# Key-value products of a linear attention: two matmuls of 64 weight columns in place of four of 32

## The chip, the cores and the metric

The kernel runs on one core of a Trainium2 chip. The metric is the time of one execution on the device in microseconds (us). A core has TensorE (PE in the profile; its weight loads are listed apart, as PEld), VectorE (DVE), ScalarE (ACT), GpSimd (POOL) and SyncE (SP), which here issues the DMA transfers. Each engine works through its own list of instructions in order and waits for the others at semaphores.

## The reference, cut to what matters

Three layers follow each other: a linear attention with exponential features, a mixer with Fourier transforms and a two-layer network, and a second mixer. The change touches the first, of which this is the core:

```python
def phi(x):
    proj = np.einsum('bhsd,df->bhsf', x, w_phi)
    proj = proj - np.max(np.abs(proj), axis=-1, keepdims=True)
    return np.concatenate([np.exp(proj), np.exp(-proj)], axis=-1)
q_p, k_p = (phi(q), phi(k))
kv = np.einsum('bhsf,bhsd->bhfd', k_p, v)
z = np.sum(k_p, axis=2)
num = np.einsum('bhsf,bhfd->bhsd', q_p, kv)
den = np.einsum('bhsf,bhf->bhs', q_p, z)[..., None] + 1e-06
return (num / den).astype(np.float32)
```

There are 4 batches, 8 heads, 576 tokens, 64 values a head, and 128 features of each sign. `kv` is the product that the change rewrites.

## The kernel before, in words

The 32 pairs of batch and head are worked off in 8 super-units `i` of four heads each: two heads stand one above the other on the partitions (index `j`), and two more along the tokens (index `u`). For each super-unit `a_load` and `a_loadv` fetch keys, queries and values. `a_proj` (L435) projects 128 tokens at a time onto the 128 features, VectorE takes the largest magnitude (L440) and subtracts it (L442), and for the keys ScalarE makes the two exponentials `ek` (L452), one for each sign `s`. `a_kv` then multiplies: the weights are `ek` of one tile of 128 tokens (128 features), the moving operand is `v` of that tile, 64 values and a column of ones that gives `z`, 65 columns. The tile that holds tokens of both heads is taken first, with 130 columns. So the first half of a super-unit (`u = 0`) makes 4 products of 130 columns and 16 of 65, the second half (`u = 1`) 16 of 65; all add up in PSUM tiles `pk`, one for each `j`. `kv_mm` (L457 to L459) is the product itself. `a_kz` copies the sums to SBUF (L486). Queries are projected likewise, turned by TensorE (L498, L510) and exponentiated (L503, L518); `a_den` (L531) makes the denominators with weights of 32 columns, `a_num` (L551) the numerators with weights of 64 columns. Behind them stand the division (`a_div`), the Fourier stages (`f_fold`, L625, L641, L673), and the layer norm `ln`, whose sum over the features is a matmul with ones (L915). From about 226 us the two networks and the second mixer follow (L1010, L1032 to L1034, L1102, L1111).

Nothing is scheduled by a compiler here: `ORDER` and `PRM` are tables that give every step a time, `at` and `later` put the steps into a heap by these times, and the heap is emptied in order. The times only set the order in which each engine gets its instructions. Steps of the weight preparation for the later layers (`w_ahead`, L718 to L781, L1564) stand among the attention's on VectorE, ScalarE, GpSimd and SyncE. When the last key-value products have released their memory, `w_fetch` (L805) loads the first network's weights.

All operands of `kv_mm` are full float32, and the compiled program executes each such matmul as two weight loads and two matmul records.

Of the kernel before, what the change touches and what calls it, by code (L numbers as in the profile page):

```python
# [270 lines left out]
def mixer_kernel(ctx: ExitStack, tc: tile.TileContext, qT, kT, vt, wphi, w11, w12, wt1, wt2, w21, w22,  # L271
                 dcos, dsin, scos, ssin, outT):
    nc = tc.nc
# [181 lines left out]
            later(V('d2', 0.8) + V('d6', 0.6) * j, sub, j)  # L455

    def kv_mm(out, e, v, first, last):  # L457
        for g in range(0, 128, 32):
            nc.tensor.matmul(out[g:g + 32], e[:, g:g + 32], v, start=first, stop=last)  # L459

    def a_kv(i, u):
        need(("v", i))
        if u:
            need(("kv", i, 0))
        elif i:
            need(("kz", i - 1, 0), ("kz", i - 1, 1))
        mark("kv", i, u)
        v, vs = T["v", i]
        if u == 0:
            T["kv", i] = [pk() for _ in range(2)]  # L470
            for j in range(2):
                for s in range(2):
                    kv_mm(T["kv", i][j][:, s * 130:s * 130 + 130], T["ek", i, j, 0][:, 0, s, :], vs[:, j], s == 0, False)
        for n in range(4):
            t = 1 + 4 * u + n
            for j in range(2):
                for s in range(2):
                    o = s * 130 + u * 65
                    kv_mm(T["kv", i][j][:, o:o + 65], T["ek", i, j, t // 4][:, t % 4, s, :], v[:, t - 1, j * 65:j * 65 + 65],
                          False, u == 1 and s == 1 and n == 3)  # L480
# [862 lines left out]
    last = {}  # L1343
# [190 lines left out]
    v = -1  # L1534
# [88 lines left out]
```

## Time and profile before

| | us |
|---|---|
| median of three runs | 1012.09 |
| the three runs | 1012.09, 1011.25, 1015.5 |
| the profiled execution | 1015.1 |
| its span, first to last instruction | 1013.4 |
| TensorE busy | 976.6 (96%) |
| VectorE, ScalarE, GpSimd busy | 694.6, 429.0, 409.4 |

The profile is of one execution. A row of the timeline gives the start, the length and the number of records merged in it, and in square brackets how long the engine had been idle before it and what ended that; "issue" is written where the wait ended with nothing that the profile shows. The view of stretches gives, for each engine, busy time and the number of its instructions. [...] Instructions themselves come from memory over DMA queues of their own, which the list of queues shows as "instruction".

### The profile page before, as it was taken

How to read it: one execution, taken by the hardware profiler on the slowest of the kernel's cores; microseconds unless marked ns; L12 is line 12 of the kernel's file. 1: busy time of each engine (PE TensorE's matmuls, PEld its weight loads, DVE VectorE, ACT ScalarE, POOL GpSimd, SP SyncE). 2: the span in 40 equal slices, each digit the busy share in tenths (PEclk: the TensorE clock that was granted, in tenths of full speed). 3: DMA queues.
4: the chain of work that ended last, by engine and by line, in shares of the span. 5: the costliest groups of instructions: out<-in, count | busy, mean ns of one | idle time of the engine just before them, and what ended most of it. 6: DMA issues, size and time to landing. Idle time of an engine off the chain costs nothing.

```text
span 1013.4 us, 23531 instructions
## 1 busy us (share of the span) xinstructions
PE 976.6 (96%) x9468; PEld 907.7 (90%) x9468; DVE 694.6 (69%) x1285; ACT 429.0 (42%) x954; POOL 409.4 (40%) x430
## 2 busy tenths in 40 slices
PE   7898999899999999999999999999999999999997
PEld 6666777579998899999999999988899999999996
DVE  5787998689689864544756753357666767766666
ACT  3676565463233422222323332234354446544442
POOL 0142223104124631523444752323266568865652
PEclk9999999899999999999999999999999999999999
DMA  8648474714445742565552498880035555754442
GB/s 283 188 138 262 134 267 155 272 40 137 169 157 178 216 163 79 197 238 181 196 170 96 162 372 334 252 293 2 1 114 170 164 177 158 244 161 146 146 146 94
DMA packets 97208, 178.66 MB, mean 176 GB/s; under 512 B 9300, under 2 KB 53268, under 8 KB 93516
## 3 DMA queue, kind: packets, MB, share of 16 engines
q1 hardware_dynamic: 97100, 177.16, 51.7%
q8 instruction: 75, 1.23, 0.5%
q14 instruction: 33, 0.27, 0.1%
HBM read 126.39 MB, written 48.31 MB: 172 GB/s over the span
## 4 chain that ended last, share of the span: by engine, by line
PE 85%; DVE 9%; issue 3%; ACT 1%; POOL 1%; DMA 0%; DVEq 0%; ACTq 0%; POOLq 0%
PE pw L1010 18%; PE pw L1102 12%; PE pz L1111 11%; PE pw L435 4%; PE pk L459 4%; PE pa L551 4%; PE pk L1033 3%; PE pk L1034 3%; PE pa L1032 3%; PE pk L1032 3%; PE pa L1034 3%; PE pa L1033 3%; PE pw L673 2%; DVE t L1564 2%; PE pa L531 2%
## 5 line engine op out<-in xcount | busy, mean ns | idle before, releaser
L1010 PE MATMUL pw<-xh,w 128*128 128x288 f32 x896 | 197.0, 295 | 0.0
L1166 DVE TENSOR_TENSOR u<-u,pz 128x576 f32<-128x576 f32 x158 | 118.9, 753 | 61.4 <-PE pz L1111 59.4
L1102 PE MATMUL pw<-x,ring 128*128 128x288 f32 x1008 | 155.4, 297 | 3.8 <-DVE f L1124 3.8
L1111 PE MATMUL pz<-g,ring 128*128 128x288 f32 x984 | 152.1, 298 | 1.5 <-DVE y L1161 1.0
L1010 PEld LDWEIGHTS pw<-xh,w 128*128 128x128 f32 x896 | 150.1, 188 | 0.5 <-DVE c L942 0.4
L1018 DVE SCALAR_TENSOR_TENSOR gl<-pw,gh 128x288 fp32r<-128x288 f32 x128 | 58.2, 455 | 132.7 <-ACT gh L1017 132.5
L1017 ACT ACTIVATE gh<-pw 128x288 fp32r<-128x288 f32 x128 | 52.6, 411 | 224.0 <-PE pw L1010 200.5
L1102 PEld LDWEIGHTS pw<-x,ring 128*128 128x128 f32 x1008 | 139.5, 188 | 7.2 <-DVE f L1124 5.2
L1111 PEld LDWEIGHTS pz<-g,ring 128*128 128x128 f32 x984 | 136.8, 188 | 5.4 <-DVE u L1166 3.5
L1010 PE MATMUL pw<-xl,w 128*128 128x288 f32 x448 | 132.3, 295 | 0.0
L1564 DVE SCALAR_TENSOR_TENSOR t<-raw,t 128x512 uint32<-128x512 uint32 (+3 forms) x130 | 101.0, 783 | 2.2
L1564 POOL TENSOR_TENSOR g<-t,g 128x288 fp32r<-128x288 f32 (+1 forms) x69 | 70.7, 1025 | 41.9 <-ACT g L1137 41.9
L1010 PEld LDWEIGHTS pw<-xl,w 128*128 128x128 f32 x448 | 84.3, 188 | 0.1
L1564 POOL TENSOR_TENSOR g<-f,g 128x288 fp32r<-128x288 f32 x69 | 56.8, 837 | 60.5 <-ACT g L1137 60.4
L1564 ACT ACTIVATE f<-f 128x288 f32<-128x288 f32 x72 | 32.0, 444 | 116.1 <-DVE f L1124 115.6
L1033 PE MATMUL pk<-gl,w 128*128 128x288 f32 x256 | 76.6, 299 | 3.3 <-DVE gl L1018 3.2
L1032 PE MATMUL pk<-gh,w 128*128 128x288 f32 x256 | 76.4, 299 | 1.7 <-DVE u L1037 0.9
L1034 PE MATMUL pk<-gh,w 128*128 128x288 f32 x256 | 76.0, 297 | 0.0
L1032 PE MATMUL pa<-gh,w 128*128 128x288 f32 x256 | 75.9, 297 | 0.0
L1034 PE MATMUL pa<-gh,w 128*128 128x288 f32 x256 | 75.7, 296 | 0.0
L1033 PE MATMUL pa<-gl,w 128*128 128x288 f32 x256 | 75.4, 294 | 0.0
L440 DVE TENSOR_REDUCE m<-pw 128x4 f32<-128x512 f32 (+1 forms) x96 | 52.5, 547 | 26.0 <-PE pw L435 25.6
(208 smaller groups left out, 2074.1 us busy)
## 6 DMA issues: line engine op xcount, KB each, us to landing
w<-wd SPq DMA_DIRECT2D x24, 1024.0 KB, 8.5
ring<-wd SPq DMA_DIRECT2D x24, 1024.0 KB, 5.5
raw<-in_w SPq DMA_DIRECT2D x32, 512.0 KB, 4.9
ring<-wd SPq DMA_DIRECT2D x24, 512.0 KB
wd<-wst SPq DMA_DIRECT2D x24, 448.0 KB, 3.5
wd<-raw SPq DMA_DIRECT2D x24, 448.0 KB, 3.7
wd<-wst SPq DMA_DIRECT2D x16, 512.0 KB, 6.6
wd<-w SPq DMA_DIRECT2D x32, 256.0 KB, 2.9
```

The source lines that it names most:

```text
L435: nc.tensor.matmul(ps[j][:, (t - t0) * 128:(t - t0 + 1) * 128], x[h], T["w"][h], start=True, stop=True)
L440: nc.vector.tensor_reduce(out=m[:, 0:n], in_=pv[j], axis=AX.X, op=ALU.max, apply_absolute_value=True)
L1010: nc.tensor.matmul(out, w[:, k, fs], x[:, k, :], start=(n == 0), stop=(n == 11))
L1017: nc.scalar.activation(out=gh, in_=out, func=AF.Relu)
L1018: nc.vector.scalar_tensor_tensor(out=gl, in0=out, scalar=0.0, in1=gh, op0=ALU.max, op1=ALU.subtract)
L1032: nc.tensor.matmul(out, wh[:, f % 4, ds], gh, start=(f == f0), stop=False)
L1033: nc.tensor.matmul(out, wh[:, f % 4, ds], gl, start=False, stop=False)
L1034: nc.tensor.matmul(out, wl[:, f % 4, ds], gh, start=False, stop=last)
L1102: nc.tensor.matmul(out, w[:, kk, hw], x[XI[i]][:, hx, kk], start=(start and k == 0), stop=(stop and k == 5), skip_group_check=(i != 2))
L1111: nc.tensor.matmul(o[s], w[:, s, hw], g[hx], start=(start and k == 0), stop=(stop and k == 2), skip_group_check=(i != 2))
L1166: nc.vector.tensor_tensor(out=u, in0=u, in1=o, op=ALU.add)
L1564: fn(*a, **k)
```

## The change

`kv_mm` issued four matmuls for each tile, each with 32 of the 128 features as weight columns and a quarter of the output's partitions; it now issues two, each with 64 features and half of the partitions. Each quarter or half sees the same moving columns and the same 128 rows. Operands, sums and the place of the products among the other steps are the same.

```diff
     def kv_mm(out, e, v, first, last):
-        for g in range(0, 128, 32):
-            nc.tensor.matmul(out[g:g + 32], e[:, g:g + 32], v, start=first, stop=last)
+        for g in (0, 64):
+            nc.tensor.matmul(out[g:g + 64], e[:, g:g + 64], v, start=first, stop=last)
```

No table of times is changed, and on every engine the steps stand in the same order as before. On TensorE this is the place of the program's last key-value products, both halves of the eighth super-unit one behind the other; x counts matmuls, without their weight loads:

```order
 L498 MATMUL pw<-ident,p 128x128 x4
 L435 MATMUL pw<-w,raw 128x128 x8
-L459 MATMUL pk<-v,ek 32x130 x16
-L459 MATMUL pk<-v,ek 32x65 x128
-L915 MATMUL pw<-s_3482,ones 128x288
+L459 MATMUL pk<-v,ek 64x130 x8
+L459 MATMUL pk<-v,ek 64x65 x64
+L915 MATMUL pw<-s_2906,ones 128x288
 L498 MATMUL pw<-ident,p 128x128 x4
 L531 MATMUL pa<-qe,kz_106 32x288 x8
```

The neighbours stay where they were (the number in the name of `s` is a running one); of the 144 matmuls between them 72 are left.

## Rows read from the trace of the kernel before

**Rows 1.** The page: busy us and instructions; instruction queue's packets, MB, share.

```profile
PE 976.6 (96%) x9468; PEld 907.7 (90%) x9468; DVE 694.6 (69%) x1285; ACT 429.0 (42%) x954; POOL 409.4 (40%) x430
...
q8 instruction: 75, 1.23, 0.5%
```

**Rows 2.** Groups, 0 to 300 us: shapes, count | busy us, mean ns | idle before.

```profile
L459 PEld LDWEIGHTS pk<-v,ek 128*32 128x32 f32 x2304 | 38.6, 112 | 9.1 <-issue 7.9
...
L459 PE MATMUL pk<-v,ek 128*32 128x65 f32 x2048 | 33.8, 223 | 6.0 <-issue 6.0
...
L551 PEld LDWEIGHTS pa<-qe,kz 128*64 128x64 f32 x256 | 16.7, 144 | 14.2 <-issue 5.3 <-ACT t L556 0.4 <-ACT kz L486 0.2
```

**Rows 3.** TensorE's waits, whole span: total us, times, longest us.

```profile
PE pk L459 <- issue: 6.0, 4, 3.1
PE pw L915 <- issue: 4.3, 1, 4.3
...
PE pw L498 <- issue: 2.3, 2, 1.6
...
PE pw L673 <- issue: 0.7, 1, 0.7
```

**Rows 4.** Stretches between ends of gaps: length, PE, PEld, DVE, ACT, POOL, clock, DMA.

```profile
19.37:24.59 5.22, 3.03 (x128) 2.65 (x128) 2.96 (x5) 2.54 (x5) 0.00 (x0) 1.00 0.96 335
...
134.65:190.35 55.70, 54.73 (x1012) 41.40 (x1013) 51.13 (x112) 36.31 (x88) 12.20 (x9) 1.00 0.56 187
190.35:196.70 6.35, 2.03 (x128) 2.05 (x129) 3.71 (x11) 1.36 (x3) 0.00 (x0) 0.90 0.99 408
```

**Rows 5.** DMA queues, 192.38 to 194.30 us: packets, MB, share of 16 engines.

```profile
q1 hardware_dynamic: 111, 0.78, 98.7%
```

**Rows 6.** DMA queues, 194.30 to 196.70 us.

```profile
q8 instruction: 1, 0.02, 2.5%
```

**Rows 7.** DMA engines' busy tenths in 40 slices of 186.0 to 188.3 us.

```profile
DMA  0000000000000000000000000000000000090000
```

**Rows 8.** Timeline of TensorE: start, length, instruction, records, idle before.

```profile
60.70 2.92 PE L459 MATMUL pk<-v,ek 128*32 128x130 f32 x160
...
66.85 2.03 PE L459 MATMUL pk<-v,ek 128*32 128x65 f32 x128
...
92.86 0.35 PE L459 MATMUL pk<-v,ek 128*32 128x65 f32 x8 [3.05 <-issue]
...
103.53 1.06 PE L641 MATMUL pw<-dcos,f 128*128 128x129 f32 x8
104.42 1.06 PE L641 MATMUL pw<-dsin,f 128*128 128x129 f32 x8
...
190.35 2.03 PE L459 MATMUL pk<-v,ek 128*32 128x65 f32 x127 [0.52 <-issue]
```

**Rows 9.** Stretches behind gaps; columns as in rows 4, the clock third from the right.

```profile
24.80:28.10 3.30, 3.30 (x74) 3.12 (x65) 0.00 (x0) 2.25 (x6) 0.00 (x0) 0.50 0.28 102
93.10:96.40 3.30, 3.30 (x22) 1.72 (x16) 2.14 (x4) 3.14 (x8) 0.00 (x0) 0.50 0.91 351
195.50:202.20 6.70, 5.50 (x30) 2.53 (x29) 1.35 (x1) 1.09 (x2) 0.00 (x0) 0.50 0.97 351
```

**Rows 10.** VectorE's waits, 0 to 100 us: total us, times, longest us.

```profile
DVE m L440 <- PE pw L435: 22.0, 9, 7.6
```

**Rows 11.** Timeline of VectorE: three instructions that it had waited for.

```profile
99.12 0.69 DVE L440 TENSOR_REDUCE m<-pw 128x4 f32<-128x512 f32 x1 [3.78 <-PE pw L435]
...
197.85 1.35 DVE L942 TENSOR_TENSOR c<-u,pw 128x1152 f32<-128x1152 f32 x1 [3.65 <-PE pw L915]
...
204.16 0.43 DVE L658 TENSOR_TENSOR yl<-pw,yh 128x258 fp32r<-128x258 f32 x1 [4.95 <-ACT yh L652]
```

**Rows 12.** Two long stretches; columns as in rows 4.

```profile
100.00:180.00 80.00, 78.88 (x1465) 60.61 (x1456) 73.04 (x162) 46.45 (x113) 19.15 (x14) 1.00 0.57 193
...
230.00:1000.00 770.00, 759.40 (x5547) 742.45 (x5545) 503.65 (x886) 292.62 (x638) 363.56 (x384) 1.00 0.51 172
```

## The prediction

> **What bounds the kernel now.** I read the totals first, then TensorE's waits, then its timeline at the longest of them, then the DMA queues and the clock there, and last VectorE, which would be next. From 230 to 1000 us TensorE is busy 759.4 of 770 us [rows 12]: behind the attention stage the kernel is bound by TensorE, and whatever TensorE gains before 230 us reaches the end if the other engines follow. In the first 200 us, where all the key-value products lie, TensorE has idle time that no operand explains. Its waits "on issue" are 6.0 us ahead of the key-value line L459, 4.3 us ahead of L915 (the first matmul behind the last key-value product), 2.3 us at L498 and 0.7 us at L673: 13.3 us in 8 gaps [rows 3]. One of them stands inside a key-value unit: 8 records are left over, and they come 3.05 us late though nothing new is needed for them [rows 8].
>
> What are these gaps? Between the end of one gap and the end of the next, TensorE executes 128 + 128 matmul and weight-load records, then elsewhere 1012 + 1013, then 128 + 129 [rows 4]; that is 256, 2025 and 257, or one, eight and one times about 254. The instruction queue of the profile moved 1.23 MB in 75 packets [rows 1], 16.4 KB each, and 2 x 9468 TensorE records over 75 packets are 252 per packet (the rest up to 256 I take for the sequencer's own waits, an estimate). So every gap ends where a new packet of instructions begins: TensorE has run out of code. The longest gap shows why. TensorE is out of instructions from 192.38 us; until 194.30 us the data queue takes 98.7% of the 16 engines and no instruction packet moves [rows 5]; between 194.30 and 196.70 us one does [rows 6], and at 196.70 us TensorE goes on. Where the DMA engines are idle it is shorter: a lone packet moves at 188.0 us (the 9 in the 36th of 40 places of a stretch of 2.3 us [rows 7]), and the block behind it begins at 190.35 us [rows 4], 2.3 us later. A block of some 254 instructions therefore has to last between about 2.7 us (some 0.4 us from the start of the block before to the packet, an estimate from the count back from 190.35 us, and these 2.3 us) and 6.4 us (190.35 to 196.70 us) if TensorE isn't to run dry.
>
> [...]
>
> Such a gap costs twice. [...] Half of that is lost: 1.65 + 1.65 + 2.75 = 6.05 us.
>
> **The change, part by part.** The order of work on every engine stays; only L459 changes. The product of one tile of 128 tokens for one head and one sign was 4 matmuls of 32 weight columns into the 4 quarters of the output partitions; now it is 2 of 64 into the halves. Each is executed in two passes, so a record is one pass of one matmul.
>
> Instructions: 2304 matmuls and 2304 loads [rows 2] are halved, 2304 fewer, 9 packets. A second-half unit was 128 + 128 = 256 instructions in 2.03 us [rows 8], a whole block in less than the least time a block needs; it becomes 128 in the same time. A first-half unit goes from 320 to 160 in 2.92 us. The neighbours are sparser, about 32 instructions per 1.1 us at most, so a block with a first-half unit lasts some 2.92 + 93/32 x 1.1 = 6.1 us. Only the last two units, which stand back to back, make 288 instructions in 4.95 us, 254 in 4.4. That lies between 2.7 and 6.4: no gap with free DMA engines, 2.0 us at the worst. I take none, because the packet concerned falls, by the count, at the same place of the program (the first microsecond of the unit at 187 us) as the one at 188.0 us, ahead of the burst [rows 7]. So 13.3 + 6.05 = 19.35 us go.
>
> Stream time: 128 records are 32 passes of 4, 63 ns a pass; 32 further records with 130 columns cost 0.89 us, 111 ns for each of 8 passes [rows 8]. All column groups see the same moving columns, so the pass of 65 columns needs at least 111/2 = 55 ns in either form. The new form has no row: a 64-column load is 144 ns long against 112 ns [rows 2], 32 ns more. One bound: fewer instructions let the pass fall to 55 ns, a gain of 8 x 512 passes = 4.1 us. The other: 32 columns more cost a load 32 ns, so 64 columns take some 64 ns, and the two loads of a pass come one behind the other, 2 x 64 = 128 ns, a loss of 65 x 512 = 33 us. The nearest row is on the side of no change: four 112 ns loads now fit into a 63 ns pass, so loads into different column groups run side by side; and at L641 a 128-column load under 129 moving columns makes a pass of (104.42 - 103.53)/8 = 111 ns [rows 8], the stream's own time, though load and stream are about as long as each other, just as 64 under 65 will be. I take 63 ns again, and 32 ns more at the start of each of some 17 runs of key-value matmuls, where the first load has no cover: +0.5 us.
>
> [...]
>
> Who is next? VectorE waited 22.0 us for projections in the first 100 us [rows 10], 7.6 of them at the start; 14.4 us can go, and TensorE gains 11.1 there (the 13.3 us of rows 3 less 4.3, 0.7 and 0.52 [rows 8] that lie behind 100 us, and 2 x 1.65). At 99.12 us VectorE idles 3.78 us against 4.7 us that TensorE gets back at that place (3.05 + 1.65); at 197.85 and 204.16 us 3.65 + 4.95 us [rows 11] against 0.5 + 4.3 + 2.75 us of TensorE's. Between 100 and 180 us it is busy 73.0 of 80 us [rows 12], so it can hardly catch up: I charge the missing 0.9 us and 0.5 us for smaller mismatches, 1.4 us.
>
> Sum: -19.35 + 0.5 + 1.4 = -17.45 us. From the profiled execution's own 1015.1 us (span 1013.4) that is 997.7 us. The three runs shown have a median of 1012.09, 3.0 us lower; as I take most of the difference for shorter gaps, which vanish anyway, I move by under 1 us: **997 us**.
>
> **Rivals.**
> Some gaps stay: a packet delayed by 4 us again meets the dense pair (2.0 us and its half clock), or one of the blocks of about 6 us, and what was gained by 100 us is partly kept by VectorE. For it: the DMA engines are as loaded. Gain 8 to 13 us: 1001 to 1006.
> VectorE takes over: its 73.0 of 80 us hold the 11 us gained before 100 us, and only the last gap with its half clock pays (0.5 + 4.3 + 2.75 = 7.6 us): 1007. Against it: its own waits for TensorE before 100 us.
> The gaps aren't code, or simply move elsewhere: 1011 to 1015. The counts speak against it.
> Slower: loads in front of their streams. The decisive point is the pass: above 63 + 17450/512 = 97 ns the kernel loses. With load and stream in turn, at least 2 x 55 = 110 ns a pass, +24 us net of 17.45: 1022; with 128 ns, 1031. Against it: the overlap seen at L459 and L641.
>
> **How the numbers follow.** Forecast (994 to 1000) 0.62; some gaps stay 0.17; VectorE 0.09, half of it on either side of 1007; no change 0.06; slower 0.06. Half a percent, what a measurement can tell from no change, is 5.06 us: the bounds are 1007.0 and 1017.2. Faster 0.62 + 0.17 + 0.04 = 0.83 (0.05 of the 0.09 counted as same), same 0.05 + 0.06 = 0.11, slower 0.06. The range runs from 989 (all 19.35 us and the 4.1 us of shorter passes, 1012.1 - 23.5) to 1008, and leaves out the last two cases.
>
> **What would show it.** In the profile after: 66 instruction packets in place of 75; no wait on issue at L459 and L915; granted clock 1.00 at the places of rows 9; a unit of 64 records with 65 columns still 2.0 us long; VectorE's waits for L435 shorter. A unit of 3 us or more would mean exposed loads; waits "on issue" at other lines, moved gaps; TensorE waiting for VectorE at L435 between 100 and 180 us, the VectorE rival. A wrong price of the 64-column load is what would hurt most.

## The result and the profile after

The changed kernel took 997.17 us (median of four runs, 996.58 to 997.74) and the kernel before 1011.85 us beside it (median of 1012.09, 1011.25, 1015.5 and 1011.6). The ratio is 0.985, with a 95% interval of 0.982 to 0.987. The profiled execution took 997.41 us, with a span of 995.5 us against 1013.4.

The page after: the span, the busy times with their instructions, and the instruction queue (packets, MB, share of 16 engines).

```profile
span 995.5 us, 21226 instructions
...
PE 971.0 (98%) x8316; PEld 906.0 (91%) x8316; DVE 694.9 (70%) x1285; ACT 428.8 (43%) x954; POOL 409.4 (41%) x430
...
q8 instruction: 65, 1.06, 0.4%
```

Against [rows 1], TensorE executes 1152 matmuls and 1152 weight loads less, from 65 packets of code in place of 75. Its busy time falls by only 5.6 us, although the span falls by 17.9: the other 12.3 us came out of idle stretches.

The groups of the key-value line in the first 300 us (shapes, count | busy us, mean ns | idle before):

```profile
L459 PEld LDWEIGHTS pk<-v,ek 128*64 128x64 f32 x1152 | 40.7, 142 | 2.2 <-issue 1.0
...
L459 PE MATMUL pk<-v,ek 128*64 128x65 f32 x1024 | 33.4, 225 | 0.0
```

Idle time ahead of the 65-column matmuls is 0.0 us; it was 6.0 [rows 2]. TensorE's waits over the whole span (total us, times, longest us), the largest three:

```profile
PE pw L1102 <- DVE f L1124: 3.8, 6, 2.3
PE pw L435 <- DVE p L442: 3.2, 4, 0.9
PE pk L1033 <- DVE gl L1018: 3.1, 4, 1.0
```

None of the waits of [rows 3] is left. In their place stands a wait that was 1.6 us before and is 3.2 now, at L435 for VectorE's subtraction L442, which frees the PSUM buffers `pw` of the projection. TensorE's timeline shows where (start, length, instruction, records, idle before):

```profile
53.93 2.98 PE L459 MATMUL pk<-v,ek 128*64 128x130 f32 x80
...
60.14 2.09 PE L459 MATMUL pk<-v,ek 128*64 128x65 f32 x64
...
85.06 1.16 PE L625 MATMUL pw<-dcos,f 128*128 128x129 f32 x8
86.96 0.48 PE L435 MATMUL pw<-w,raw 64*128 64x128 f32 x2 [0.73 <-DVE p L442]
88.35 1.19 PE L435 MATMUL pw<-w,raw 64*128 64x128 f32 x14 [0.91 <-DVE p L442]
89.47 4.52 PE L459 MATMUL pk<-v,ek 128*64 128x130 f32 x80
93.92 1.16 PE L625 MATMUL pw<-dcos,f 128*128 128x129 f32 x8
...
95.57 1.06 PE L641 MATMUL pw<-dcos,f 128*128 128x129 f32 x8
...
178.35 4.84 PE L459 MATMUL pk<-v,ek 128*64 128x130 f32 x144
183.12 0.75 PE L915 MATMUL pw<-s,ones 128*128 128x288 f32 x2
...
209.51 0.40 PE L1010 MATMUL pw<-xh,w 128*128 128x288 f32 x1
```

The units of [rows 8] are as long as they were: 2.98 us against 2.92, and 2.09 against 2.03. The last two units (178.35 us) run through, and L915 follows without a gap. Stretches at the places of [rows 9] and over the long stage (length, PE, PEld, DVE, ACT, POOL, granted clock as a share of full speed, DMA share, GB/s):

```profile
89.40:92.70 3.30, 3.30 (x45) 3.24 (x46) 3.23 (x7) 1.16 (x3) 0.00 (x0) 0.50 0.20 71
...
178.40:183.10 4.70, 4.70 (x146) 4.65 (x144) 4.56 (x11) 2.22 (x8) 1.47 (x1) 1.00 0.48 135
195.50:202.20 6.70, 6.70 (x56) 3.93 (x55) 5.46 (x15) 5.31 (x10) 0.14 (x1) 1.00 0.15 52
213.00:983.00 770.00, 759.38 (x5553) 742.11 (x5551) 504.62 (x886) 293.24 (x639) 364.19 (x384) 1.00 0.51 172
```

Behind the attention the program is the same: TensorE is busy 759.38 of 770 us, as in [rows 12]. The unit behind the new waits (89.47 us) runs at a granted clock of 0.50 up to 92.7 us and takes 4.52 us in place of 2.98.

**Where the 17.9 us of span came from.** These are rows of the kernel before at the same places of the program, which were not shown ahead:

```profile
96.84 1.16 PE L625 MATMUL pw<-dcos,f 128*128 128x129 f32 x8
...
99.02 2.92 PE L459 MATMUL pk<-v,ek 128*32 128x130 f32 x160
...
225.76 0.40 PE L1010 MATMUL pw<-xh,w 128*128 128x288 f32 x1
...
1006.61 1.75 PE L1111 MATMUL pz<-g,ring 128*128 128x288 f32 x12
```

and of the kernel after, TensorE's last run of matmuls:

```profile
989.44 1.75 PE L1111 MATMUL pz<-g,ring 128*128 128x288 f32 x12
```

| place in the program | before, us | after, us | gained so far |
|---|---|---|---|
| first-half unit [rows 8] | 60.70 | 53.93 | 6.77 |
| L625, behind the gap of 3.05 us | 96.84 | 85.06 | 11.78 |
| the next L459 | 99.02 | 89.47 | 9.55 |
| L641 [rows 8] | 103.53 | 95.57 | 7.96 |
| L915, behind the last unit [rows 4] | 196.70 | 183.12 | 13.58 |
| first L1010 | 225.76 | 209.51 | 16.25 |
| last run of matmuls, L1111 | 1006.61 | 989.44 | 17.17 |
| last instruction | 1013.4 | 995.5 | 17.9 |

Up to L625 11.78 us are gained, between L641 and L915 5.62, and behind L915 2.67: 20.07 us. From L625 to L641 3.82 us are given back: 2.23 where TensorE waits for VectorE (0.73 + 0.91 us idle; the rest goes to running the projection in two pieces), and 1.59 in the unit at half clock. Of the last 1.65 us, 0.73 lie behind TensorE's last run of matmuls, where VectorE finishes the last results and they are stored (6.8 us to the end before, 6.1 after). The other 0.92 come with a stretch of the kernel before behind the attention (columns as above):

```profile
342.30:345.50 3.20, 3.09 (x13) 3.09 (x14) 3.10 (x7) 1.19 (x2) 0.73 (x2) 0.50 0.81 298
```

There the granted clock was 0.50 for some 3.4 us; the profile after has no such stretch. It comes and goes in kernels of either form: in the profiles of all thirteen runs TensorE waits 0.9 us at this place (L1032) and then 1.0 us (L1033), and the granted clock falls behind these waits in six of them. Among the six are one of the two profiles of the kernel before and two of the changed kernel with an edit more (the five transfers and, the second time, the six matmuls below).

### The profile page after: what moved, and what is told of

The parts are those of the page before. It is cut to its first block, busy times and chain, and to the rows that moved or that the text cites. A ratio compares the mean times of both kernels' runs of the same rounds, so it can differ in the third digit from the quotient of the medians.

```text
span 995.5 us, 21226 instructions
## 1 busy us (share of the span) xinstructions
PE 971.0 (98%) x8316; PEld 906.0 (91%) x8316; DVE 694.9 (70%) x1285; ACT 428.8 (43%) x954; POOL 409.4 (41%) x430
## 4 chain that ended last, share of the span: by engine, by line
PE 78%; DVE 10%; issue 2%; ACT 2%; POOL 1%; DMA 1%; SPq 0%; DVEq 0%; POOLq 0%; ACTq 0%
PE pw L1010 18%; PE pw L1102 12%; PE pz L1111 11%; PE pk L1033 3%; PE pk L1034 3%; PE pk L1032 3%; PE pa L1032 3%; PE pa L1034 3%; PE pa L1033 3%; DVE t L1564 3%; PE pw L673 2%; PE pa L551 2%; PE pk L459 2%; PE pw L435 2%; PE pw L625 1%
## 5 line engine op out<-in xcount | busy, mean ns | idle before, releaser
L1010 PE MATMUL pw<-xh,w 128*128 128x288 f32 x896 | 196.9, 295 | 0.0
L1111 PE MATMUL pz<-g,ring 128*128 128x288 f32 x984 | 152.2, 298 | 1.5 <-DVE y L1161 1.0
L1010 PEld LDWEIGHTS pw<-xh,w 128*128 128x128 f32 x896 | 149.8, 188 | 0.5 <-issue 0.4
L1111 PEld LDWEIGHTS pz<-g,ring 128*128 128x128 f32 x984 | 136.8, 188 | 5.3 <-DVE u L1166 3.1
L1010 PE MATMUL pw<-xl,w 128*128 128x288 f32 x448 | 132.2, 295 | 0.0
L1010 PEld LDWEIGHTS pw<-xl,w 128*128 128x128 f32 x448 | 84.2, 188 | 0.1
L1033 PE MATMUL pk<-gl,w 128*128 128x288 f32 x256 | 76.4, 299 | 3.3 <-DVE gl L1018 3.1
L1032 PE MATMUL pk<-gh,w 128*128 128x288 f32 x256 | 76.3, 298 | 1.7 <-DVE u L1037 0.9
L1032 PE MATMUL pa<-gh,w 128*128 128x288 f32 x256 | 75.7, 296 | 0.0
L1033 PE MATMUL pa<-gl,w 128*128 128x288 f32 x256 | 75.1, 294 | 0.0
```

The source lines that it names most:

```text
L1010: nc.tensor.matmul(out, w[:, k, fs], x[:, k, :], start=(n == 0), stop=(n == 11))
L1032: nc.tensor.matmul(out, wh[:, f % 4, ds], gh, start=(f == f0), stop=False)
L1033: nc.tensor.matmul(out, wh[:, f % 4, ds], gl, start=False, stop=False)
L1111: nc.tensor.matmul(o[s], w[:, s, hw], g[hx], start=(start and k == 0), stop=(stop and k == 2), skip_group_check=(i != 2))
```

## Experiments: does the instruction supply make the gaps?

The theory is that TensorE runs out of code in the dense units of 32-column matmuls. The first four kernels ran on one chip beside 19 runs of the kernel before, with a median of 1013.91 us (1009.28 to 1023.82).

**Only the last super-unit with 64 columns** (a part of the change alone; the number `i` of the super-unit is handed to `kv_mm`, not shown):

```diff
-        for g in range(0, 128, 32):
-            nc.tensor.matmul(out[g:g + 32], e[:, g:g + 32], v, start=first, stop=last)
+        w = 64 if i == 7 else 32
+        for g in range(0, 128, w):
+            nc.tensor.matmul(out[g:g + w], e[:, g:g + w], v, start=first, stop=last)
```

> Kernel before, but the eighth super-unit alone multiplies with 64 weight columns. Up to 186 us the program is the same instruction for instruction, so the gaps up to there stay. Theory (TensorE runs out of code): the 288 instructions of the last two units need 4.4 us for a block instead of 2, the gaps of 0.52 and 4.32 us and the 2.75 us of half clock behind them go, 7.6 us: about 1004.3 us against a median of 1011.9. Rival (the 64-column form is quicker in itself, everywhere alike): an eighth of the 14.7 us gained, 1.8 us: about 1010.

Measured: 1007.66 us (ten runs, 1001.75 to 1014.21), ratio 0.994 [0.990, 0.997], so 6.3 us less (2.6 to 10.5 by the interval; the rival's 1.8 lies outside). TensorE's timeline in this kernel:

```profile
29.46 2.03 PE L460 MATMUL pk<-v,ek 128*32 128x65 f32 x127 [0.51 <-issue]
36.91 1.01 PE L499 MATMUL pw<-ident,p 128*128 128x128 f32 x4 [5.42 <-issue]
...
188.50 4.84 PE L460 MATMUL pk<-v,ek 128*64 128x130 f32 x144
```

The dense pair (188.50 us) has lost its gaps, and there are still gaps before 100 us. Four of the six stand at the same records as before, with other lengths: the one at 36.91 us was 1.65 us in the first profile of the kernel before and is 5.42 here. Two short ones (0.51 us at 29.46, 0.23 us at 67.60) are at places where that profile has none.

**All but the last super-unit with 64 columns** (the diff is against the kernel ahead):

```diff
-        w = 64 if i == 7 else 32
+        w = 32 if i == 7 else 64
```

> The other half: seven super-units with 64 columns, the eighth with 32 as before. Theory (code): no gap before 175 us; then the 576 instructions of the last two units make two blocks of 2.0 us each. The first needs at least 2.7 us (gap of some 0.7 us), the second falls into the weight loads and needs about 6.4 us (gap of some 4.4 us with 2.75 us of half clock): 7 to 8 us slower than the changed kernel, about 1005 us. Rival (form quicker in itself): seven eighths of the gain, about 999 us.

Measured: 1002.68 us (1002.3 to 1005.38), ratio 0.988 [0.984, 0.993], 11.2 us less. By the theory it should have been some 7 us less than the kernel before, by the rival some 13: the time lies between and does not decide. The two parts sum to 17.5 us; the whole change gave 14.7 on another chip. TensorE's timeline:

```profile
179.76 2.03 PE L460 MATMUL pk<-v,ek 128*32 128x65 f32 x128 [0.31 <-issue]
186.50 0.53 PE L460 MATMUL pk<-v,ek 128*32 128x65 f32 x15 [4.72 <-issue]
```

These are the only waits "on issue" left, and both are inside the unit that kept 32 columns. So in these two kernels the gaps go where the instruction count is halved, and only there. The spread goes with them, though from few runs: 3 us here in four, 12 us in ten where the early units kept 32 columns.

**The kernel before, with the burst behind the last unit put off:** two loads of the first network's weights take a later place in the table of times.

```diff
-w_fetch/0/0 204.420
+w_fetch/0/0 207.951
-w_fetch/0/1 205.750
+w_fetch/0/1 207.952
```

> Kernel before with 32 columns everywhere; only the 4 MB of weight loads (L805) that start at 188.4 us stand some transfers later in SyncE's list, so that they start at about 208 us. Theory (the packet of code waits behind the data in the DMA engines): the packet for the block at L915 moves at once, the gap there is at most 1 us in place of 4.32, and the half clock of 195.5 to 202.2 us goes at least in part: 3 to 6.5 us quicker, 1005.5 to 1009 us. Rival (the gap is set by L915's operand or by the number of instructions alone): the gap stays at 4.3 us, 1012 us; late weights could cost TensorE a wait at L1010.

Measured: 1012.45 us (ten runs, 1005.93 to 1016.27), ratio 0.997 [0.994, 1.0005]. The median is 1.5 us lower, where 3 to 6.5 was expected; the time does not resolve the edit, and the spread between runs is wide enough to cover it. The trace does show it, in TensorE's timeline:

```profile
192.57 2.03 PE L459 MATMUL pk<-v,ek 128*32 128x65 f32 x127 [0.52 <-issue]
196.18 0.65 PE L915 MATMUL pw<-s,ones 128*128 128x288 f32 x2 [1.58 <-issue]
```

and in the stretch behind it (columns as above):

```profile
195.50:202.20 6.70, 6.02 (x54) 4.37 (x54) 3.39 (x7) 2.45 (x7) 0.00 (x0) 1.00 0.01 2
```

The gap ahead of L915 is 1.58 us in place of 4.32, and no half clock follows. From the start of one block to the next it takes 3.6 us (196.18 - 192.57) in place of 6.4. So the data transfers made most of this gap; without the burst it shrinks, but stays, because 2.03 us of work do not last for these 3.6 us.

**One matmul of 128 weight columns** (instructions halved once more):

```diff
-        for g in (0, 64):
-            nc.tensor.matmul(out[g:g + 64], e[:, g:g + 64], v, start=first, stop=last)
+        nc.tensor.matmul(out, e, v, start=first, stop=last)
```

> One matmul of 128 weight columns in place of two of 64: half the instructions again, the same number of passes. [...] Rival (loads are hidden whatever their width): as the changed kernel, 997 us.

Measured: 1029.47 us (1021.49 to 1031.44), ratio 1.012 [1.005, 1.019]: slower, and above the 1018 to 1025 that the author's estimate gave (a pass of 111 ns, as at L641 [rows 8], in all 512), though its profile has no wait "on issue" either. TensorE's timeline, and under it two stretches:

```profile
15.85 8.82 PE L458 MATMUL pk<-v,ek 128*128 128x130 f32 x40
...
37.77 4.58 PE L458 MATMUL pk<-v,ek 128*128 128x130 f32 x40
...
53.87 3.68 PE L458 MATMUL pk<-v,ek 128*128 128x65 f32 x32
```

```profile
16.00:36.00 20.00, 20.00 (x110) 19.54 (x112) 6.97 (x14) 7.02 (x15) 0.00 (x0) 0.50 0.43 158
40.00:60.00 20.00, 19.62 (x204) 14.84 (x202) 15.53 (x33) 12.57 (x30) 3.19 (x7) 1.00 0.63 200
```

The pass of 65 columns now takes 3.68/32 = 115 ns. By the same division it takes 2.03/32 = 63 ns with four matmuls and 2.09/32 = 65 ns with two. So the chance that the prediction gave to an exposed load was about the right effect in the wrong form: one undivided load of 128 columns costs the pass some 50 ns, and two halves cost nothing measurable. 115 ns is also what a 128-column load takes under 129 moving columns (111 ns at L641 [rows 8]), so the pass goes at the load's pace. Load and stream do overlap: with 130 columns the pass of this kernel takes (4.58 - 3.68)/8 = 112 ns, no more than with 65, and in turn they would take longer with the longer stream. Nor do the loads of the changed kernel stand in front of their streams, as the slow rival has it: by its estimate a pass would then take at least 110 ns, and it takes 65.

Some 8 to 10 us of this kernel's loss are something else: from 16 to 36 us the granted clock is 0.50, while TensorE is busy all 20 us. A unit takes 8.82 us there and 4.58 us at full clock. The one run with a mean clock of 0.996 took 1021.49 us; the other three, at 0.986 to 0.988, took 1029 to 1031.

**The kernel before, profiled again,** on another chip.

> The kernel before, a second profile. Theory (gaps end where a packet of code arrives, and arrival depends on what the DMA engines carry): the gaps stand at the same records, blocks of some 254 instructions apart, but have other lengths and number, and their sum with the half clock behind them explains the difference to the first profile. Rival (gaps from operands): same places and same lengths.

Measured: 1019.79 us, span 1018.1. TensorE's waits "on issue" in it (total us, times, longest us):

```profile
PE pk L459 <- issue: 6.6, 4, 3.5
PE pw L915 <- issue: 4.3, 1, 4.3
PE pw L498 <- issue: 3.7, 2, 3.0
PE pw L673 <- issue: 0.9, 1, 0.9
```

That is 15.5 us in 8 gaps against 13.3 in [rows 3]. Seven of the eight places are the same, and the lengths are not: the one that was 3.05 us at 92.86 us [rows 8] is 2.10 here. The gap of 0.19 us at 19.37 us is missing, and one of 0.50 us stands elsewhere. A count that the prediction made for three stretches holds for all: in the two profiles of the kernel before and in those of the first and the third experiment above, TensorE's matmuls and weight loads between the ends of any two neighbouring gaps are a whole multiple of a number from 250 to 257. So the gaps stand only where one packet ends and the next begins, but not every packet has a gap, and which of the smaller ones show differs from one execution to the next.

## Experiments: what the new waits cost

VectorE is late at 87 us in the changed kernel. Its timeline there (start, length, instruction, idle before):

```profile
79.89 0.76 DVE L598 TENSOR_TENSOR e<-u 128x576 f32<-128x576 f32 x1 [2.28 <-DMA u<-t]
89.34 0.69 DVE L440 TENSOR_REDUCE m<-pw 128x4 f32<-128x512 f32 x1 [0.77 <-PE pw L435]
```

and the same instruction in the kernel before:

```profile
86.66 0.76 DVE L598 TENSOR_TENSOR e<-u 128x576 f32<-128x576 f32 x1 [2.38 <-DMA u<-t]
```

VectorE waits as long for the rearranged values `u` in both. Before, TensorE then stood still for 3.05 us and ran at half clock for 3.3, and VectorE caught up: at 99.12 us it waited for TensorE [rows 11].

**The changed kernel with five transfers put behind the ones for `u`** (three loads of keys, two steps of the weight preparation):

```diff
-a_load/5/k/1 81.370
+a_load/5/k/1 93.170
-a_load/6/k/0 83.260
+a_load/6/k/0 93.180
-a_load/6/k/2 93.080
+a_load/6/k/2 93.190
-w_ahead/128/512#7 90.380
+w_ahead/128/512#7 93.200
-w_ahead/128/512#4.1.4.2 91.380
+w_ahead/128/512#4.1.4.2 93.210
```

> Changed kernel; three key loads that are needed 60 us later, one weight load and one weight store stand behind the two divisions' stores of u in SyncE's list. What is left of waits in the changed kernel starts, by the theory, at VectorE's wait of 2.28 us for u at 79.9 us, which makes TensorE wait 0.73 and 0.91 us at L435 and the clock fall at 89.3 us. Theory: u lands 1.5 to 3 us earlier, VectorE's wait goes, TensorE's two waits and the half clock behind them go: 1.5 to 3.3 us quicker than the changed kernel, 994 to 995.7 us. Rival (VectorE is simply full there, or the transfer is late for another reason): no difference, 997 us.

Measured: 1005.59 us (ten runs, 1003.58 to 1009.09) beside 1012.82 for the kernel before, ratio 0.993 [0.991, 0.995]: worse than the change alone. VectorE's wait for `u` is gone, but the moved store of prepared weights (`wd<-wst`) now comes late for ScalarE, and TensorE waits for ScalarE; VectorE in turn waits 6.65 us for the denominators. ScalarE's and TensorE's timelines:

```profile
85.79 0.62 ACT L766 CAST wst<-t 128x512 fp32r<-128x512 f32 x1 [9.53 <-DMA wd<-wst]
...
87.90 2.19 PE L551 MATMUL pa<-qe,kz 128*64 128x288 f32 x8 [7.64 <-ACT dd L536]
```

The cast at L766 could not write its buffer before the store had read it, and the copy of the denominators (L536) was queued behind that cast.

The next three kernels shared a chip with seven runs of the kernel before (median 1018.62 us; the ratios leave out the longest, 1025.04). **The changed kernel once more** gave 995.83 us (995.46 to 999.47), ratio 0.978 [0.973, 0.983], with the same 3.1 us of waits at L435.

> The changed kernel once more, as the yardstick for the two others on the same chip. Theory: no gap on issue, hence a spread of about 1 us between executions, 996.5 to 998 us, while the kernel before spreads by 10 us and more, as its gaps differ from one execution to the next.

**Only the three loads of keys moved** (the first six lines of the diff above).

> Changed kernel; only the three key loads that are needed 60 us later stand behind the two stores of u in SyncE's list, while the weight load and the weight store keep their places (the store held back ScalarE 9.5 us when it was moved). Theory (VectorE's wait for u at 79.9 us makes TensorE wait at L435 and the clock fall at 89.3 us): u lands 1 to 2 us earlier, VectorE's 2.28 us shrink by as much, TensorE's 0.73 + 0.91 us and the 1.7 us of half clock go: 994 to 996 us. Rival (VectorE is full there whatever the store does): 997 us.

Measured: 996.61 us (995.29 to 999.03), ratio 0.979 [0.973, 0.984]. Its timeline of TensorE:

```profile
87.09 1.16 PE L435 MATMUL pw<-w,raw 64*128 64x128 f32 x14 [0.25 <-DVE p L442]
88.17 3.29 PE L459 MATMUL pk<-v,ek 128*64 128x130 f32 x80
...
986.86 1.76 PE L1111 MATMUL pz<-g,ring 128*128 128x288 f32 x12
```

and the last of these rows in the change alone, on this chip:

```profile
989.52 1.75 PE L1111 MATMUL pz<-g,ring 128*128 128x288 f32 x12
```

The wait for VectorE is 0.25 us and the unit is back at 3.29 us, but the time is that of the change alone. In these profiles the gain is not lost on TensorE: its last run of matmuls starts 2.7 us earlier. Behind it, finishing and storing the last results takes 7.8 us in this profile and 8.3 in that of the change alone, against 6.1 us in nine of the thirteen; whether the runs without a profile had such long ends is not known.

**Six matmuls more near the start**, in the place where TensorE waits for the first projections; nothing reads their results:

```diff
+    def a_fill(n):
+        ps = pa()
+        for _ in range(n):
+            nc.tensor.matmul(ps[:, 0:128], T["ones"], T["ones"], start=True, stop=True)
+    at(1.1, a_fill, 3)
+    at(2.2, a_fill, 3)
```

> Changed kernel with six more matmuls on ones, whose result nobody reads, in two of TensorE's waits among the first projections (10 to 13 us); all else is the same. Theory (the clock falls at 14.3 us because TensorE stood idle in these waits): the half clock of 14.3 to 17.7 us goes, up to 1.7 us quicker, 995.5 us. Rival (the waits of VectorE behind set the pace there anyway): 997 us.

Measured: 994.39 us (994.2 to 994.81), ratio 0.976 [0.971, 0.981]; its four runs lie below the four of the change alone by 0.6 us at least. The first key-value unit, at 15.82 us in the changed kernel, shows why:

```profile
15.82 3.86 PE L459 MATMUL pk<-v,ek 128*64 128x130 f32 x80
```

and with the six matmuls:

```profile
12.88 0.94 PE L416 MATMUL pa<-ones 128*128 128x128 f32 x6
...
15.47 2.97 PE L464 MATMUL pk<-v,ek 128*64 128x130 f32 x80
```

**Both edits, and the six matmuls alone again,** on another chip (five runs each, beside 1014.66 us for the kernel before):

> The changed kernel with both earlier edits: three loads of later super-units put behind the place where VectorE waits at 80 us, and six extra matmuls on ones near the start whose results nothing reads. If the two half-speed stretches (14.3 and 89.4 us) cost what the rows say, both are gone and the time is 1.5 to 3 us below the changed kernel without them, near 993 to 994.5 us. Rival: the loads alone moved the time by under 0.8 us, because VectorE gives the gain back behind 90 us; then this run equals the one with the filler alone, within 0.5 us.

> The filler alone once more, on the same chip as the kernel with both edits: 994.4 us as before, and by the theory 0.5 to 1.5 us above it; by the rival level with it.

Measured: both edits 997.45 us (997.22 to 998.83), ratio 0.983 [0.981, 0.986]; the six matmuls alone 996.22 us (995.24 to 997.26), ratio 0.982 [0.979, 0.985]. The theory wanted both edits to be the faster; they were 1.2 us slower. The stretches behind the two places, of the kernel with both edits:

```profile
14.40:17.60 3.20, 3.20 (x30) 2.98 (x30) 2.96 (x7) 2.46 (x7) 0.00 (x0) 0.53 0.95 322
89.80:93.00 3.20, 3.20 (x46) 3.20 (x48) 3.13 (x7) 1.46 (x4) 0.00 (x0) 0.50 0.18 63
```

Both half-clock stretches are back, and VectorE waited again, 1.93 us for the denominators in place of 2.28 for `u`. With the six matmuls alone neither stretch was there, in both profiles (granted clock 1.00 from 14.4 to 17.6 and from 89.4 to 92.7 us). VectorE's wait at this place is not fixed by the order of the loads: in the two profiles of the six matmuls alone, one program, it was 2.17 us for `u` and 0.65 for the denominators. Nor does the clock follow from TensorE's wait: in the first of them TensorE waited 0.63 and 0.91 us here, and the granted clock stayed at 1.00. So what moving the loads is worth, and how the six matmuls act on the clock at 89 us, far behind them, is not settled. Where the plain change ran beside them, no kernel beat it by more than 1.4 us.

## Why the prediction was right, and where it was not

997 us was forecast and 997.17 measured. The mechanism held, and so did the size of its main term. That the sum came out within 0.2 us is luck: the term for VectorE was 2.4 us too small, and two things that come and go in kernels of either form, with a somewhat larger gain, made up for it.

- **Gaps are missing code, and halving the instructions removes them.** Right: no wait "on issue" is left in the profile after, 65 packets against 66 forecast, and the two partial kernels lose just the gaps of the part that was changed. That the sequencer's own waits fill a packet up to 256 was an estimate: with the semaphore waits that the traces list in TensorE's own queue, 228 and 227, there are 255.5 records for each of the 75 packets before and 259.4 for each of the 65 after.
- **The size, 19.35 us.** 20.07 us by the table, with 11.78 against 11.07 up to L625 (6.37 by the unit at 60.70 us and 4.70 at the gap), 5.62 against 5.52 (0.68 + 0.52 + 4.32) up to L915, and 2.67 against 2.75 behind it. This term was sized well. Its part of 6.05 us takes half of TensorE's busy time at the granted clock of 0.50 [rows 9] for lost. The runs show about that: matmuls of 288 columns start 0.24 us apart at 0.50 (from 342.8 us in the kernel before) and 0.13 us apart at 1.00 (from 347.0 us), and a unit of the kernel with 128 columns takes 8.82 us at 0.50 and 4.58 at 1.00.
- **No gap at the dense pair.** Right: 288 records in 4.84 us ran through, in the profile after and in the kernel where only this pair was changed. The least time of a block, 2.7 us, was an estimate; the shortest cycle seen behind a dense unit was 3.6 us, which decides the same way (254 of the 288 records last 4.3). In the profile after, a lone packet of code moves at 178.6 us, while no data moves, and the burst of data begins at 181 us: the packet does come ahead of it, as argued.
- **The price of the 64-column pass.** Right: 65 ns where 63 was taken. With 128 columns it is 115 ns, between the two bounds and past the decisive 97. The start of a run costs 0.06 us instead of 0.032 (2.98 against 2.92, 2.09 against 2.03), so some 16 runs cost 1.0 us where 0.5 stood.
- **The mismatch with VectorE, 1.4 us.** This is the step that failed: 3.82 us were given back, at L435 some 87 us into the profile, and a stretch of half clock stood behind the waits. The step compared VectorE's idle time at one instruction (3.78 us [rows 11]) with the gain at that place. That idle time stood behind the projection; the buffers that the projection needs are freed by VectorE's L442 ahead of it. VectorE's wait of 2.4 us for `u`, a line below [rows 10] in the same view, was not read. In the kernel before, TensorE stood still for code in the meantime (3.05 us), and no wait for VectorE shows there. "Granted clock 1.00 at the places of rows 9" holds for the first and the third, not for this one. VectorE's own waits for L435 in the first 100 us fell from 22.0 to 13.6 us, as forecast.
- **What made up for it:** 0.92 us with the half-clock stretch at 342 us and 0.73 us at the end of the kernel, which the sum did not contain and which come and go in kernels of either form, and the 0.7 us of the term above. So -20.07 (net of the dearer run starts) + 3.82 - 0.92 - 0.73 = -17.9, where the sum had -17.45.
- **The level of the kernel before.** Moving less than 1 us from the profiled execution's sum was right, for the reason given: the gaps differ from one execution to the next. Within one set of runs the kernel before ranged over 4.3 us (four runs) to 14.5 (19 runs), the changed one over 1.2 and 4.0 (four runs each).

The slow rival (loads in front of their streams) fell with the 65 ns; its time (1022 to 1031) came with one matmul of 128 columns, but there too load and stream overlap. The VectorE rival was right in kind, at 3.8 us and not at 11, and not where it looked: between 100 and 180 us TensorE did not wait for VectorE at L435.

## What to carry to other kernels

Count TensorE's instructions per microsecond as well as its columns: where a run of small matmuls uses up a packet of code (here some 254 records) in less than the 3.6 to 7.5 us that passed here from the start of one such packet to the start of the next, merge column groups, as long as the pass stays as short (here 65 ns with two column groups and 63 with four, but 115 with one). Waits "on issue" that end whole multiples of one number of records apart (here 250 to 257), with a count of packets to match, are the sign of it. When a gap closes, look at what it covered on the other engines: each of their waits in the microseconds ahead of it, and not only those for the engine that gains.

## What the runs showed of the hardware

- Five gaps before 140 us came at the same records in all four profiles of kernels with 32 columns there, but with lengths from 0.2 to 5.4 us; others of 0.2 to 0.7 us came and went. With them came a spread of up to 14.5 us between runs of one program (19 runs), against 1.2 and 4.0 us without (four runs each).
- While data filled 98.7% of the DMA engines, no code moved for 1.9 us [rows 5]; one packet came in the next 2.4 us [rows 6], in which data still filled them (100.2%). Putting off two loads cut that gap from 4.32 to 1.58 us.
- With 128 weight columns in one piece a pass took 111 to 115 ns, whether 65, 129 or 130 columns moved; with two or four pieces in different column groups the 65-column pass took 63 to 65 ns.
- The granted clock stayed at 0.50 for 20 us while TensorE was busy all the time, in the kernel with 128 weight columns; it had waited 0.7 to 0.9 us three times ahead of that, as in the changed kernel, where 3.4 us at 0.50 followed. Why it lasted was not tried.
